# Gated linear attention, then a mixture of experts: key halves on array quarters, and forward scans that begin with reciprocals

## The chip, the core and the metric

The kernel runs on one core of a Trainium2 chip. A core has a matrix engine (TensorE, PE in the tables), a vector engine (VectorE, DVE), a scalar engine (ScalarE, ACT), a general engine (GpSimd, POOL) and a queue that only issues transfers (SyncE, SP). Each runs its own list of instructions in order, and they wait for each other through semaphores. The metric is the time of one execution on the device in microseconds: before the change the median of three runs is 389.31 us (389.28 to 391.26). All data is 32-bit floating point unless a sentence says otherwise.

## What is computed

First a gated linear attention over 4 batches, 8 heads, 768 steps and heads of 48, then a hierarchical mixture of 16 experts over the 3072 resulting rows.

```python
for t in range(S):
    state = alpha[:, :, t, :, None] * state + np.einsum('bhd,bhe->bhde', k[:, :, t], v[:, :, t])
    y[:, :, t] = np.einsum('bhd,bhde->bhe', q[:, :, t], state)
...
g_idx = np.argmax(x @ w_group, axis=1)      # one of 4 groups, then one of its 4 experts
...
h = np.maximum(xg[mask_e] @ w1[g, e], 0.0)
out[tok_idx] = combined[:, None] * (h @ w2[g, e])
```

The recurrence is computed in chunks of 128 steps. Within a chunk the keys are multiplied by the product of the decays that still follow them (a scan that runs backwards gives these products), the queries by the product of the decays so far (a scan that runs forwards), and the causal part of queries times keys, times the values, gives the chunk's own share. A state of 48 by 48 for each head carries the rest from chunk to chunk. Since both factors are counted towards the chunk's end, the queries have to be divided by the product over the whole chunk.

## The kernel before

There are 24 chunks (4 batches of 6). The 8 heads lie in 4 pairs: a pair fills 112 partitions, one head on 0 to 47, the other on 64 to 111. The host has the inputs laid out so. The inputs come in 11 units of one, two or three chunks, each cut in two or four parts; for the later batches a part is one pair over three chunks, so its rows are 3 x 128 = 384 elements long (387 with a boundary element for each chunk). A part of two chunk-pairs has 256 (258).

For each part (names as the planner has them):

- R, `back` (L378): the backward scan on DVE. Its second operand is a column of ones in PSUM (`one_col`).
- KP, `decayed` (L414): keys times the scan, on POOL, or on DVE where `BY_DVE` (L709) lists the part.
- F, `forth` (L388): the forward scan on DVE. Its second operand is `starts`, a tile that occupies a whole PSUM bank: 3e38 everywhere but 1.0 at the chunks' beginnings, so that a multiply followed by a minimum begins anew with each chunk.
- W, `wholes` (L395, L396): for each unit a reciprocal of the whole-chunk products and a minimum.
- QS, `queries` (L405): ACT multiplies the queries by that reciprocal, one instruction for each pair and chunk, 128 elements each.
- QP (L414): scaled queries times the forward scan, on POOL or DVE.

For each chunk, on PE:

- SC, `scores` (L428): 8 products of 128 keys by 128 queries, contraction 48, into two PSUM banks.
- masks: head set by head set, either DVE multiplies the PSUM bank by a triangle of ones (`masked`, L433), or ACT copies the bank to SBUF (L856) and POOL blanks the upper triangle (`mask`, L437). `MASKS` (L891) says how many of the two DVE takes.
- OUT, `outputs` (L506): masked scores times values, contraction 128, on top of FB, `from_before` (L494): queries times the state.
- G, `gains` (L463), with the keys turned by TR (L446): what the chunk adds to the state; DVE adds it (L472) and ACT scales it (L479).
- ROWS, `to_rows` (L527): the outputs turned to rows, with the router's logits beside them.

Then DVE chooses the experts for groups of chunks, and POOL scatters each chunk's 128 rows to the experts' slots with one indirect DMA (X, L625). When all rows are there, the experts run one after the other: L237 is the first matrix product, L248 the second. The rows of a job are fetched by SP, turned on DVE (L1031), and the results sent out by POOL (L1023).

The order of instructions on each engine is fixed when the program is built. `in_turns` (L35) is a list scheduler: every piece of work has an engine, a duration that was written in by hand, the pieces that it needs and a due time; the engines' queues are filled in the order it finds. PE's pieces are in a fixed sequence of their own. `FIRST` and `STEP` (L704) set the due times of the chunks, `X0` and `XSTEP` (L892) those of the scatters, `QUEUE` (L788) the order of SP's transfers: L a unit's inputs, V values, W the weights of ROWS, B the filling of the slots. `cq`, the forward scan's result, has three buffers, so a forward scan waits until the product QP three parts earlier has read its buffer.

Of the kernel before, what the change touches and what calls it, by code (L numbers as in the profile page):

```python
# [12 lines left out]
F32 = mybir.dt.float32  # L13
# [9 lines left out]
P = 128  # L23
# [11 lines left out]
def in_turns(works, free):  # L35
# [19 lines left out]
    while len(turns) < len(works):  # L55
# [7 lines left out]
        for w in sorted((w for t, w in can if t <= now + 1e-9), key=lambda w: w.due):  # L63
            if not any(now < t < now + w.takes - 0.4 and y.due < w.due and y.due < now + w.takes
                       for t, y in can):
                w.start, free[e] = now, now + w.takes
                left[e].remove(w)
                turns.append(w)
                break
# [27 lines left out]
def gla_then_hierarchical_moe(  # L97
# [71 lines left out]
    def bank():  # L169
# [9 lines left out]
    causal = cp.tile([P, P], F32, name="causal")  # L179
    nc.gpsimd.memset(causal, 1.0)  # L180
    nc.gpsimd.affine_select(out=causal, in_=causal, pattern=[[1, P]], compare_op=ALU.is_ge,
                            fill=0.0, base=0, channel_multiplier=-1)
# [78 lines left out]
    nc.vector.memset(starts[0:R, 0:UC * A1:A1], 1.0)  # L261
# [7 lines left out]
    with ExitStack() as gla:  # L269
# [42 lines left out]
        for kind, u, i, n in blocks_of(units, HP):  # L312
            begins[kind, u, i] = at
            at += P * width_of(kind, n)

# [67 lines left out]
        def forth(u, i):  # L383
# [5 lines left out]
                out=cq, data0=a[:, 0:n * A1], data1=starts[0:R, 0:n * A1], initial=1.0,  # L389
                op0=ALU.mult, op1=ALU.min)  # L390

        def wholes(u):
            k = units[u][2]
            ready["whole", u] = w = sp.tile([R, HP, UC], F32, name="whole")
            nc.vector.reciprocal(out=w[:, :, 0:k], in_=ready["rev", u][:, :, :, 0])  # L395
            nc.vector.tensor_tensor(out=w[:, :, 0:k], in0=w[:, :, 0:k],  # L396
                                    in1=starts[0:R, 1:2, None].to_broadcast([R, HP, k]),
                                    op=ALU.min)

        def queries(u, i):  # L400
            n, q, _, _ = of_unit(u, i)
            k, g = units[u][2:]
            for j in range(n):
                c = j % k
                nc.scalar.activation(out=q[:, j, :], in_=q[:, j, :], func=AF.Copy,  # L405
                                     scale=ready["whole", u][:, i * g + j // k, c:c + 1])

        def decayed(kind, u, i, engine):
# [3 lines left out]
            else:  # L412
                of, by = q, ready.pop(("cq", u, i)).rearrange("r (c s) -> r c s", c=n)
            engine.tensor_tensor(out=part_of(kind, u, i, P), in0=of, in1=by[:, :, 1:A1],  # L414
                                 op=ALU.mult)

        def side(p, i):

            c = (i + p + 1) % 2
            return slice(64 * c, 64 if c == 0 else R)  # L420

        def scores(n):
            u, c = where[n]
            qp, kp = ready["qp", u], ready["kp", u]
            z = [pairs.tile([P, HP, P], F32, name=f"zs{i}") for i in range(2)]
            for p in range(HP):
                for i, r in enumerate(heads):
                    nc.tensor.matmul(z[i][:, p, :], lhsT=kp[r, p, c, :],  # L428
                                     rhs=qp[r, p, c, :], start=True, stop=True)
            return z  # L430

        def masked(sm, z, i):
            nc.vector.tensor_tensor(out=sm[:, i], in0=z[i], in1=causal[:, None, :]  # L433
                                    .to_broadcast([P, HP, P]), op=ALU.mult)

        def mask(sm, i):
            nc.gpsimd.affine_select(  # L437
                out=sm[:, i], in_=sm[:, i], pattern=[[0, HP], [1, P]],
                compare_op=ALU.is_ge, fill=0.0, base=0, channel_multiplier=-1)
# [43 lines left out]
        def of(z, p):  # L483
            return z[:, p % 2, p // 2 * P:(p // 2 + 1) * P]

        def from_before(n, st):
# [4 lines left out]
            for p in range(HP):  # L491
                for i, r in enumerate(heads):
                    o = side(p, i)
                    nc.tensor.matmul(of(z, p)[o], lhsT=st[r, p, 0:o.stop - o.start],  # L494
                                     rhs=qp[r, p, c, :], start=(p < 2), stop=False,
# [3 lines left out]
        def outputs(n, sm, z):  # L499
# [3 lines left out]
            for i in range(2):  # L503
                for p in range(HP):
                    h, o = 2 * p + i, side(p, i)
                    nc.tensor.matmul(of(z, p)[o],  # L506
# [799 lines left out]
```

## Time and profile before

The profiled execution took 390.5 us, of which 388.8 us are the span from its first instruction to its last. The table is taken from that execution.

| row of the profile | instructions | busy us | mean ns |
|---|---|---|---|
| PE, all | 3366 | 374.7 | |
| PE, experts, L237 and L248 | 1536 | 252.8 | 325 |
| PE, scores L428 | 384 | 28.2 | 285 |
| PE, outputs L506 | 384 | 27.2 | 280 |
| DVE, all | 420 | 162.4 | |
| DVE, mask of 512 elements from PSUM, L433 | 28 | 18.3 | 679 |
| DVE, forward scans L388 of 387 elements (w, qka) | 16 and 8 | 15.0 and 7.5 | 945, 947 |
| DVE, forward scans L388 of 258 elements (qka, w) | 6 and 6 | 4.1 and 4.0 | 677, 674 |
| ACT, all | 379 | 139.3 | |
| ACT, scaling of queries L405 (w, qka) | 60 and 36 | 19.8 and 11.7 | 402, 407 |
| ACT, copies of scores L856 | 20 | 11.0 | 576 |
| POOL, all | 240 | 195.3 | |
| POOL, blanking of 512 elements L437 | 20 | 12.5 | 637 |

Each f32 matrix product appears as two instructions, so the 8 products of a chunk's scores are 16. The busy time of PE counts the whole latency of overlapping instructions, so a busy PE says little about how much of the array is used; the distance from one group's start to the next says more. The granted clock of PE is 0.992 of full speed over the span.

The attention takes the first 117 us or so of the span and the experts almost all of the rest: the last OUT starts at 115.17 us, the first full expert job (216 columns) at 141.47 us, and the last expert's second product ends at about 378 us.

### The profile page before, as it was taken

What the parts mean: (1) busy time and instruction counts of PE and PEld (TensorE: products, weight loads), DVE (VectorE), ACT (ScalarE), POOL (GpSimd) and SP (SyncE); (2) the same over time, 40 slices, a digit from 0 to 9 for tenths busy, and PEclk for the clock granted to TensorE, in tenths of its full rate; (3) what the DMA queues carried; (4) which work ended last, traced back from release to release, by engine and by line L of the source; (5) the groups of instructions that cost most, each with busy time, mean ns of one, the idle gap of its engine ahead of it and who ended that gap; (6) DMA issues with size and microseconds to landing.
All of it is one profiled execution on the core that took longest, in us unless ns stands there. A gap on an engine that the chain in (4) does not pass through costs nothing.

```text
span 388.8 us, 8864 instructions
## 1 busy us (share of the span) xinstructions
PE 374.7 (96%) x3366; PEld 356.6 (92%) x3366; DVE 162.4 (42%) x420; ACT 139.3 (36%) x379; POOL 195.3 (50%) x240
## 2 busy tenths in 40 slices
PE   8999999999999899999999999999999999999990
PEld 3888998898989899999999999999999999999990
DVE  7999998899868220207322020220201202202200
ACT  5989899596762211111121121211212112112110
POOL 5988886888746321244261633526336235144341
PEclk9999999999999999999999999999999999999996
DMA  8999999994313799986585866768668777665000
GB/s 284 380 410 412 413 358 352 410 417 172 100 64 128 154 328 346 333 244 219 175 255 218 276 220 207 224 227 282 227 201 257 269 245 240 249 250 182 16 22 27
DMA packets 32411, 95.22 MB, mean 245 GB/s; under 512 B 18175, under 2 KB 18454, under 8 KB 27888
## 3 DMA queue, kind: packets, MB, share of 16 engines
q1 hardware_dynamic: 27552, 85.10, 63.5%
q0 software_dynamic: 4816, 9.55, 7.3%
q8 instruction: 27, 0.44, 0.5%
q14 instruction: 16, 0.13, 0.1%
HBM read 79.47 MB, written 15.56 MB: 244 GB/s over the span
## 4 chain that ended last, share of the span: by engine, by line
PE 69%; DMA 18%; issue 5%; POOL 4%; SPq 1%; DVE 1%; POOLq 0%; ACT 0%; DVEq 0%; ACTq 0%
PE bank L237 29%; PE bank L248 29%; DMA slots_d<-blank 7%; DMA qka<-in_qka_dram 5%; DMA w<-in_qka_dram 3%; PE zo L506 3%; PE zs L428 3%; PE bank L527 2%; DMA out_dram<-yq,dst_q 2%; POOL out_dram L1023 1%; DMA v<-in_v_dram 1%; PE zo L494 1%; SPq L320 1%; POOL slots_d L625 1%; PE bank L446 1%
## 5 line engine op out<-in xcount | busy, mean ns | idle before, releaser
L1023 POOL DMA_INDIRECT out_dram<-yq,dst_q x99 | 96.4, 974 | 153.2 <-DVE yq L1019 121.3
L237 PE MATMUL bank<-xt_e,w 128*128 128x128 f32 (+15 forms) x768 | 126.5, 325 | 1.4 <-DVE dst_q L1045 0.8
L248 PE MATMUL bank<-hT,w 128*128 128x128 f32 (+15 forms) x768 | 126.3, 324 | 0.0
L237 PEld LDWEIGHTS bank<-xt_e,w 128*128 128x128 f32 x768 | 124.1, 190 | 1.7 <-PE bank L248 0.9
L248 PEld LDWEIGHTS bank<-hT,w 128*128 128x128 f32 x768 | 124.1, 190 | 0.0
L1040 DVE CAST dst_q<-xq 128x7 int32<-128x7 f32 (+2 forms) x16 | 2.7, 168 | 168.8 <-DMA out_dram<-yq,dst_q 168.8
L239 ACT ACTIVATE hT<-bank 128x256 f32<-128x256 f32 (+15 forms) x64 | 31.3, 489 | 96.3 <-PE bank L237 96.3
L250 ACT COPY yT<-bank 128x256 f32<-128x256 f32 (+31 forms) x32 | 12.7, 398 | 109.0 <-PE bank L248 109.0
L625 POOL DMA_INDIRECT slots_d<-xr,place x24 | 24.1, 1002 | 10.6 <-issue 3.3
L506 PE MATMUL zo<-sm,v 128*48 128x128 f32 (+1 forms) x384 | 27.2, 280 | 1.0 <-POOL sm L437 1.0
L428 PE MATMUL zs<-qp,kp 48*128 48x128 f32 x384 | 28.2, 285 | 0.0
L527 PE MATMUL bank<-wr,yt 112*128 112x116 f32 x192 | 26.1, 279 | 0.5 <-ACT sm L856 0.5
L506 PEld LDWEIGHTS zo<-sm,v 128*48 128x48 f32 (+1 forms) x384 | 20.3, 129 | 6.5 <-POOL sm L437 2.4
L428 PEld LDWEIGHTS zs<-qp,kp 48*128 48x128 f32 x384 | 23.4, 187 | 2.6 <-DVE qp L414 0.8
L527 PEld LDWEIGHTS bank<-wr,yt 112*128 112x128 f32 x192 | 23.3, 191 | 0.9 <-ACT sm L856 0.7
L405 ACT ACTIVATE w<-w,whole 112x128 f32<-112x128 f32 x60 | 19.8, 402 | 2.0 <-DMA w<-in_qka_dram 2.0
L378 DVE TENSOR_TENSOR_SCAN rev<-w,starts 112x387 f32<-112x387 f32 (+1 forms) x22 | 18.5, 869 | 3.4 <-DMA w<-in_qka_dram 3.4
L414 POOL TENSOR_TENSOR kp<-w,rev 112x384 f32<-112x384 f32 (+1 forms) x21 | 18.3, 886 | 2.2 <-DVE rev L378 2.0
L414 POOL TENSOR_TENSOR qp<-w,cq 112x384 f32<-112x384 f32 (+1 forms) x20 | 17.1, 862 | 4.4 <-ACT w L405 3.9
L433 DVE TENSOR_TENSOR sm<-zs,causal 128x512 f32<-128x512 f32 x28 | 18.3, 679 | 2.4 <-PE zs L428 2.2
L388 DVE TENSOR_TENSOR_SCAN cq<-w,starts 112x387 f32<-112x387 f32 (+1 forms) x22 | 19.1, 871 | 0.0
L1016 DVE STREAM_TRANSPOSE yq<-yT 128x672 f32<-128x672 f32 (+2 forms) x15 | 12.3, 818 | 15.5 <-ACT yT L250 15.4
(135 smaller groups left out, 340.6 us busy)
## 6 DMA issues: line engine op xcount, KB each, us to landing
w<-in_w_dram SPq DMA_DIRECT2D x32, 1536.0 KB, 7.1
w<-in_qka_dram SPq DMA_DIRECT2D x16, 578.0 KB, 10.4
slots_d<-blank SPq DMA_DIRECT2D x4, 1372.0 KB, 19.1
qka<-in_qka_dram SPq DMA_DIRECT2D x8, 578.0 KB, 12.7
v<-in_v_dram SPq DMA_DIRECT2D x3, 1152.0 KB, 15.8
xq<-slots_d SPq DMA_DIRECT2D x32, 85.8 KB, 7.6
qka<-in_qka_dram SPq DMA_DIRECT2D x6, 385.5 KB, 6.3
xq<-slots_d SPq DMA_DIRECT2D x28, 73.5 KB, 6.3
```

Source lines behind the costliest of these rows:

```text
L237: nc.tensor.matmul(z[:, k * n:(k + 1) * n], lhsT=w1[:, dc, f * P:(f + 1) * P], rhs=xt[:, dc, 0:n], start=(dc == 0), stop=(dc == DC - 1))
L239: return lambda: nc.scalar.activation(out=hT[:, f0:f0 + 2, 0:n], in_=z[:, 0:2 * n].rearrange("p (f t) -> p f t", f=2), func=AF.Relu)
L248: nc.tensor.matmul(z[:, i * n:(i + 1) * n], lhsT=w2[:, f, dc * P:(dc + 1) * P], rhs=hT[:, f, 0:n], start=(f == 0), stop=(f == FC - 1))
L378: nc.vector.tensor_tensor_scan(out=part_of("rev", u, i, A1).rearrange("r c s -> r (c s)")[:, ::-1], data0=a[:, W:0:-1], data1=one_col.to_b ...
L388: nc.vector.tensor_tensor_scan(out=cq, data0=a[:, 0:n * A1], data1=starts[0:R, 0:n * A1], initial=1.0, op0=ALU.mult, op1=ALU.min)
L405: nc.scalar.activation(out=q[:, j, :], in_=q[:, j, :], func=AF.Copy, scale=ready["whole", u][:, i * g + j // k, c:c + 1])
L414: engine.tensor_tensor(out=part_of(kind, u, i, P), in0=of, in1=by[:, :, 1:A1], op=ALU.mult)
L428: nc.tensor.matmul(z[i][:, p, :], lhsT=kp[r, p, c, :], rhs=qp[r, p, c, :], start=True, stop=True)
L506: nc.tensor.matmul(of(z, p)[o], lhsT=vs[b][:, bc, h * D:h * D + o.stop - o.start], rhs=sm[:, i, p, :], start=(p < 2 and bc == 0), stop=Tru ...
L527: nc.tensor.matmul(z[:, at:at + W], lhsT=yt[:, p, :], rhs=wr[:, p, :], start=(p == 0), stop=(p % 2 == 1), skip_group_check=True)
L625: dma = nc.gpsimd.indirect_dma_start(out=slots_by[cs.start + c], out_offset=bass.IndirectOffsetOnAxis(ap=it["to"][:, c:c + 1], axis=0), in ...
L1023: nc.gpsimd.indirect_dma_start(out=out_by.popleft().rearrange("n (j w) -> (n j) w", j=4), out_offset=bass.IndirectOffsetOnAxis(ap=dst[:, b ...
```

## The change

Seven things are changed together.

1. SC computes the keys of a chunk in two halves of 64. The first pass multiplies one half with all 128 queries, the second the other half with the last 64 queries alone; the quarter of the scores that is always zero is not computed. Each product uses 64 rows and 64 columns of the array, and four neighbouring products in the order lie on four different quarters.
2. The scores of a head set now take 384 columns of a bank: 256 whose keys and queries belong to the same half (they need the triangle), then 128 that need none. Masks multiply the 256 alone, on DVE or on POOL (a product with the triangle in place of the blanking), and ACT copies the rest.
3. OUT too is done by key halves on quarters, with a `drain` of PE before the first pass (where FB came before it) and between the two passes.
4. The queries are no longer scaled: QS goes, and W writes reciprocals for two parts at a time into `begun`, a new SBUF tile that takes the place of `starts` as the second operand of the forward scans. So a forward scan begins with the reciprocal, and now needs W, and W the backward scans of its parts.
5. G moves behind ROWS, next to FB; before it stood behind OUT.
6. The layout follows: values of half of the heads come with the two halves of a chunk swapped, keys of those parts are written with the halves swapped, and the pairs are distributed over the two output banks in another way.
7. The plan is new: other durations, `MASKS`, `BY_DVE`, `QUEUE`, groups, due times, and 0.2 in place of 0.4 in a rule of the scheduler. Eight products KP and QP lie on DVE in place of four. The fill B 0 now goes ahead of unit 7's inputs, and unit 8's inputs come after the values V 2.

The core of the diff:

```diff
-    causal = cp.tile([P, P], F32, name="causal")
+    HB, HS = P // 2, HP // 2
+    halves = [slice(0, HB), slice(HB, P)]
+    causal = cp.tile([P, HB], F32, name="causal")
...
-    nc.vector.memset(starts[0:R, 0:UC * A1:A1], 1.0)
...
+        begun = buf.tile([R, 2, UC * A1], F32, name="begun")
+        nc.vector.memset(begun, HUGE)
...
             nc.vector.tensor_tensor_scan(
-                out=cq, data0=a[:, 0:n * A1], data1=starts[0:R, 0:n * A1], initial=1.0,
+                out=cq, data0=a[:, 0:n * A1], initial=1.0,
+                data1=begun[:, i % 2, 0:n * A1],
                 op0=ALU.mult, op1=ALU.min)
...
-        def wholes(u):
-            k = units[u][2]
-            ready["whole", u] = w = sp.tile([R, HP, UC], F32, name="whole")
-            nc.vector.reciprocal(out=w[:, :, 0:k], in_=ready["rev", u][:, :, :, 0])
...
-        def queries(u, i):
...
-                nc.scalar.activation(out=q[:, j, :], in_=q[:, j, :], func=AF.Copy,
-                                     scale=ready["whole", u][:, i * g + j // k, c:c + 1])
+        def wholes(u, j):
+            _, _, k, g = units[u]
+            of = ready["rev", u][:, 2 * g * j:2 * g * (j + 1), :, 0]
+            nc.vector.reciprocal(out=begun[:, :, 0:g * k * A1:A1],
+                                 in_=of.rearrange("r (i g) c -> r i (g c)", g=g))
...
+        def by_quarters(j):
+            for m in range(HS):
+                for p in (m, m + HS) if j == 0 else (m + HS, m):
+                    yield p, slice(0, P) if j == 0 else halves[1], lies(p, j)
...
-            z = [pairs.tile([P, HP, P], F32, name=f"zs{i}") for i in range(2)]
-            for p in range(HP):
-                for i, r in enumerate(heads):
-                    nc.tensor.matmul(z[i][:, p, :], lhsT=kp[r, p, c, :],
-                                     rhs=qp[r, p, c, :], start=True, stop=True)
+            z = pairs.tile([P, 2, 512], F32, name="zs")
+            for j in range(2):
+                for p, qs, x in by_quarters(j):
+                    for i, r in enumerate(heads):
+                        nc.tensor.matmul(blocks(z[x, i, 0:3 * HS * HB], p, j),
+                                         lhsT=kp[r, p, c, x],
+                                         rhs=qp[r, p, c, qs].rearrange("r (a q) -> r a q", q=HB),
+                                         start=True, stop=True)
...
+        def only_earlier(engine, to, z):
+            k = z.shape[1]
+            to, z = (t[:, :, 0:OWN].rearrange("s i (a q) -> s i a q", q=HB) for t in (to, z))
+            engine.tensor_tensor(out=to, in0=z, in1=causal[:, None, None, :]
+                                 .to_broadcast([P, k, 2 * HS, HB]), op=ALU.mult)
...
+            for j in range(2):
+                if j or bc:
+                    nc.tensor.drain()
+                for p, qs, x in by_quarters(j):
+                    for i in range(2):
+                        h, o = 2 * p + i, side(p, i)
+                        nc.tensor.matmul(of(z, p)[o, qs].rearrange("r (a q) -> r a q", q=HB),
+                                         lhsT=vs[b][x, bc, h * D:h * D + o.stop - o.start],
+                                         rhs=blocks(sm[x, i], p, j),
...
-            add(f"W{u}", DVE, 0.34, 0.42, partial(wholes, u), each("R", u),
+            for j in range(parts(u) // 2):
+                add(f"W{u}.{j}", DVE, 0.2, 0.28, partial(wholes, u, j),
+                    each("R", u)[2 * j:2 * j + 2], before_it("F", u, 2 * j))
...
-        QUEUE = [('L', 1), ('V', 0, 0, 1), ('L', 2), ('L', 3), ('W',), ('V', 0, 1, 3), ('L', 4), ('V', 0, 3, 6), ('L', 5), ('L', 6), ('V', 1, 0, 6), ('L', 7), ('L', 8), ('V', 2, 0, 6), ('B', 0), ('B', 1), ('B', 2), ('B', 3), ('L', 9), ('V', 3, 0, 6), ('L', 10)]
+        QUEUE = [('L', 1), ('V', 0, 0, 1), ('L', 2), ('W',), ('V', 0, 1, 3), ('L', 3), ('L', 4), ('V', 0, 3, 6), ('L', 5), ('L', 6), ('V', 1, 0, 6), ('B', 0), ('L', 7), ('V', 2, 0, 6), ('L', 8), ('B', 1), ('B', 2), ('B', 3), ('L', 9), ('V', 3, 0, 6), ('L', 10)]
...
-        MASKS = [1, 0, 0, 1, 1, 1, 0, 2, 0, 0, 1, 1, 1, 2, 1, 2, 2, 2, 2, 2, 2, 2, 1, 1]
+        MASKS = [1, 1, 0, 1, 1, 1, 0, 0, 1, 1, 1, 1, 1, 1, 2, 2, 2, 2, 2, 2, 2, 1, 1, 1]
```

## The prediction, made before the changed kernel had run

> **What bounds the kernel now.** I read the page first, then the chain of waits, PE's timeline, and busy time by stretches. The experts fill PE from 141 us on and the change touches none of them. What is at stake is the attention, up to about 117 us. From 75 us on the chain of waits there is PE alone, one group after another, and earlier PE's timeline shows the same groups with gaps of 0.7 us at most. One chunk on PE:
>
> ```profile
> 105.58 0.66 PE L494 MATMUL zo<-qp,state 48*48 48x128 f32 x16
> 106.17 1.09 PE L506 MATMUL zo<-sm,v 128*48 128x128 f32 x16
> 107.08 0.64 PE L463 MATMUL bank<-v,kt 128*48 128x48 f32 x16
> 107.64 1.16 PE L428 MATMUL zs<-qp,kp 48*128 48x128 f32 x16
> 108.74 0.60 PE L446 MATMUL bank<-ident,kp 112*128 112x112 f32 x4
> 109.18 1.06 PE L527 MATMUL bank<-wr,yt 112*128 112x116 f32 x8
> 110.17 0.74 PE L494 MATMUL zo<-qp,state 48*48 48x128 f32 x16
> ```
>
> Start to start: FB 0.59, OUT 0.91, G 0.56, SC 1.10, TR 0.44, ROWS 0.99, together 4.59 us. OUT runs from 9.74 us (chunk 0) to 115.17 us (chunk 23), 4.58 us a chunk: PE sets the pace. But the others have little room (columns: stretch, its length, then PE, PE's weight loads, DVE, ACT, POOL, each busy us with its count):
>
> ```profile
> 5.00:20.00 15.00, 14.48 (x185) 10.79 (x185) 14.57 (x36) 12.15 (x36) 12.98 (x25) 1.00 1.03 386
> 20.00:60.00 40.00, 39.67 (x631) 34.97 (x628) 38.29 (x76) 36.44 (x113) 33.51 (x43) 1.00 1.02 396
> 60.00:101.00 41.00, 40.30 (x641) 35.92 (x643) 37.29 (x97) 31.20 (x96) 33.58 (x37) 1.00 0.80 311
> ```
>
> DVE is busy 90.2 of these 96 us, POOL 80.1, with 15.9 us of gaps. The preparation (scans and products) ends here: the last QP ends at 100.9, and SC of chunk 21, the first that needs it, starts at 102.9, so the lead is 2.0 us.
>
> **PE.** Within a group the trace has one quarter of the array taking a 128-column matmul each 0.109 us (FB: 105.724, 105.834, 105.943). Streaming alone is then FB 4 x 0.109 = 0.44, OUT 8 x 0.109 = 0.87, G 0.47, SC 8 x 0.112 = 0.89, TR 0.39, ROWS 0.89, sum 3.95. The missing 0.64 lies at the four places where the array changes its shape (ROWS to FB, FB to OUT, G to SC, SC to TR): 0.16 each. After: SC and OUT each have 4 x 0.109 in the first pass and 4 x 0.058 in the second (G's pitch for 64 weight columns), 0.67, so streaming is 3.53. FB, OUT and SC share one shape, and three changes remain: 0.48. Two drains come. Neither occurs before: at least 0.16 each, as a change of shape empties the array too; at most 0.32, if a drain also waits for the modelled end (272 ns of a matmul less its 109 ns) before that. I take 0.24. Sum 3.53 + 0.48 + 0.48 = 4.49, a gain of 0.10 a chunk, **2.4 us** over 24; by the ends 6 us gained or 1.4 us lost.
>
> Here a rule speaks against the change. The Trainium skill, "TensorE: Matmul & The Clock Gate", section "Wait — 56ns, not 53.3ns?", says that starts of matmuls never come closer than about 25 ns, however small. SC and OUT become 32 instructions each: 0.80 in place of 0.67, 0.26 a chunk, 6 us in all, and the gain is a loss of 3.8. The row says otherwise where quarters differ: FB's first four start at 105.578, .584, .591 and .598, 7 ns apart. G's 16 take 28 ns each, but there weights set the pitch. I take the row.
>
> **ACT.** QS goes: 19.8 + 11.7 = 31.5 us. Copies of scores were 11.0; now 14 of 384 elements (the row of XR, 0.48), 3 of 768 (0.84, the row of the 784-element copy), 14 of 128 (about 0.28, between EX's 60 elements at 0.26 and 192 at 0.33) and 7 of 256 (0.385) give 15.9. Net -26.6 us, and none of it on the path at once; what it removes are POOL's waits for ACT's queries, 3.9 + 2.1 = 6.0 us.
>
> **DVE.** Masks 18.3 us become 14 of 256 (0.40, the DVE product's row) and 7 of 512 (0.68): 10.4. Reciprocals: 10 pairs, 3.5 us, become 18 of about 0.19: 3.4. Products: four more, +1.6. `begun`'s memset (0.7) lies in the 1.6 us before the first input. Net -6.4 us, worth nothing while PE sets the pace.
>
> **POOL.** Own work up to the last QP: 48 products of 384 at 0.895 (two in a row took 1.79) = 43.0, 16 of 256 at 0.64 = 10.2, masks 11 x 0.64 + 3 x 1.25 = 10.8 (POOL has no such row; its product of 256 is nearest, doubled for 512), 13 scatters ahead of that QP in the new order at 1.19 (12.30 us for 12, and 0.16 gaps) = 15.5, constants 0.6. Sum 80.1, as before.
>
> **The forward scans' second operand.** It moves from PSUM to SBUF, and this is what I think decides. Columns: start, duration.
>
> ```profile
> 59.18 0.95 DVE L388 TENSOR_TENSOR_SCAN cq<-w,starts 112x387 f32<-112x387 f32 x1
> 59.31 0.95 POOL L414 TENSOR_TENSOR kp<-w,rev 112x384 f32<-112x384 f32 x1
> ...
> 14.90 0.64 POOL L414 TENSOR_TENSOR kp<-w,rev 112x256 f32<-112x256 f32 x1
> 15.44 0.40 DVE L414 TENSOR_TENSOR qp<-w,cq 112x256 f32<-112x256 f32 x1
> 15.49 0.93 POOL L414 TENSOR_TENSOR kp<-w,rev 112x256 f32<-112x256 f32 x1
> ```
>
> A scan with its second operand in PSUM and a POOL product run side by side, each at its usual time. But where DVE runs a product with both inputs in SBUF, POOL's product of 0.64 takes 0.93: it stood for 0.29 of the 0.34 us that the two overlap. At 24.27 the other order shows: POOL's product runs, and DVE's takes 0.58. The Trainium skill, "SBUF — State Buffer", section "Who interferes with whom", states it as a rule: a DVE instruction with two SBUF inputs contends with a GpSimd instruction that reads SBUF, and the later one waits until the earlier has finished. By the rule every scan holds POOL for its whole length; by the row for 0.85 of the overlap.
>
> The scans' pitch is 0.875 (24 wide) and 0.61 (12): 28.3 us, and eight DVE products bring 2.9, together 31.2. By the row's 0.85 that is 26.5, by the rule 31.2; I take the row. Scatters read no rows on POOL that the scan could hold, as far as the trace tells, and the 7.6 us of scans that fall among scatters (69 to 101) lie beside them half of the time: 3.8 free. **22.7 us** remain to be served one after the other. POOL's gaps were 15.9, of which 6.0 went with QS; its longest one (3.25 us, up to 69.2) is the first scatter waiting for the fills to land, which a later POOL meets already landed, so most of the other 9.9 vanish too, and I leave 2. The last QP then ends at 4.9 (first product) + 80.1 + 22.7 + 2 = 109.7 against 100.9: +8.8. Less the lead of 2.0 that is eaten first, and 0.3 for three faster chunks after it: **+6.5 us** at the end of the attention. DVE suffers too: a scan finds POOL at work two times in three and waits some 0.4, and with three `cq` buffers it also waits for the delayed QP; its own 6.4 us pay for that.
>
> **Ends of the attention.** The first SC needs QP of the second part, at 7.9 us before; in the new order POOL's QP of the first part stands against the second scan and a DVE product, and it comes at 7.5 to 8: nothing. Behind the last OUT the chain is gates, last scatters, rows, expert 0; it follows the last OUT, so a shift of that one arrives whole. SP: fill B 0 (1.4 MB, 3.5 us at 390 GB/s) now stands ahead of unit 7's inputs, which landed at 40.4 and are scanned at 44.7; V 2 and it delay unit 8's by 6.5, scanned at 52.5 but used at 76. Neither reaches PE; without that lead it would be 3.5 us.
>
> **Sum.** 389.3 + 6.5 = **395.8 us** for the median; the profiled execution, 390.5 with a span of 388.8, would be near 397.
>
> **Rivals.**
>
> - *Faster: PE keeps the pace.* Scans don't hold POOL, or the holds fall into gaps that lie ahead of need (units 6 to 9 were ready 3 to 6 us early). For it: 15.9 us of gaps and a lighter DVE. Then 389.3 - 2.4 = 386.9; with the cheap drain 383.1. It decides if less than 14 of the 22.7 us remain: the last QP then comes by 100.8, when a PE that gained 0.10 a chunk is ready for it (102.9 less 2.1). Chance 0.27.
> - *No difference:* the hold eats the lead and PE's gain, 387.4 to 391.3. Chance 0.13 with the weak end of my forecast.
> - *Much slower: DVE and POOL hold each other,* by the whole rule, with all 9.9 us of gaps kept: +4.7 + 7.9 on top, 408. Against it: they would have to miss every gap. Chance 0.05 above 403.
> - *The change doesn't do what it says:* quarters run two at a time. SC becomes 16 x 0.109 / 2 + 16 x 0.058 / 2 = 1.34, OUT the same, +0.67 each, 32 us: 421. FB's four at once speak against it. Chance 0.01.
>
> My forecast holds 0.54, from 391.3 to 403. Within 0.5% (1.9 us) I call no difference, which is about what a measurement of this kernel can tell. Slower 0.60, same 0.13, faster 0.27. Range 385 to 403: 0.12 lie below it, 0.06 above.
>
> **What would show it.** Right: L388's scans or POOL's products grow from their usual 0.95 and 0.92 to 1.2 and more where they overlap; the last QP ends near 110; PE has gaps before SC that end at a product. Wrong: those rows stay, and PE's chunk is 4.5 us or less throughout. PE's part alone: SC start to next start near 0.83, OUT to SC near 0.91. If PE's chunk without waits is above 4.6, the drains cost over 0.3 each and the first rival falls too.

## The result: 5.3% slower, and the profile after

The changed kernel takes 411.95 us (median of four runs, 407.02 to 414.40) against 389.29 us before; the ratio is 1.053, with an interval of 1.045 to 1.061. The forecast was 395.8 us: the sign was right, the size less than a third of it. The profiled execution took 414.4 us, of which 412.3 us are the span: 23.5 us more than before. It was the slowest of the four and counts as a slow one, with a mean clock of 0.961; the other three took 407.0 to 412.1 us at 0.965 to 0.983, so what is read from the clock below holds for this one execution. All of the added time lies in the attention. OUT of the last chunk starts at 138.88 us in place of 115.17, and behind it the experts take the time that they took. A chunk now takes 5.60 us in place of 4.58.

The same stretches as before (stretch, length, then PE, PE's weight loads, DVE, ACT, POOL, each busy us with its count; then the granted clock, the busy share of the DMA engines, GB/s):

```profile
5.00:20.00 15.00, 11.46 (x236) 8.37 (x235) 13.40 (x29) 4.88 (x14) 8.55 (x16) 1.00 1.03 378
20.00:60.00 40.00, 33.97 (x728) 27.87 (x728) 35.93 (x69) 21.86 (x63) 35.86 (x36) 0.96 1.02 399
60.00:101.00 41.00, 37.95 (x675) 31.39 (x674) 27.11 (x63) 17.32 (x51) 26.63 (x27) 0.71 0.73 272
```

Two things are new. PE is no longer busy all the time, though nobody else is busier: between 60 and 101 us DVE fell from 37.3 to 27.1 us and POOL from 33.6 to 26.6. And the clock of PE, 1.00 in the whole attention before, is 0.96 and 0.71. The row of the page that gives it in 40 slices of the span (9 is 90% or more) shows where:

```profile
PEclk9999895589999999999999999999999999999997
```

By the trace's record of the clock it is at half speed from 41.8 to 45.2 us and from 62.2 to 86.1 us, and full elsewhere in the attention. At half speed a chunk on PE takes some 6.4 to 6.8 us.

The step that the forecast took as decisive is there, and as large as forecast:

```profile
L396 DVE TENSOR_TENSOR_SCAN cq<-w,begun 112x387 f32<-112x387 f32 x16 | 20.1, 1273 | 0.0
L419 POOL TENSOR_TENSOR qp<-w,cq 112x384 f32<-112x384 f32 x16 | 18.2, 1148 | 3.7 <-DVE cq L396 2.7 <-DVE lg L560 0.9
L419 POOL TENSOR_TENSOR kp<-w,rev 112x384 f32<-112x384 f32 x16 | 17.9, 1126 | 5.2 <-DVE rev L386 5.2
```

These forward scans of 387 elements last 1.27 us in place of 0.945 (the eight that read another tile 1.44 in place of 0.947), these products of POOL 1.13 to 1.15 in place of 0.92 to 0.94, while the backward scans, which still read PSUM, stay at 0.93. All forward scans together take 40.8 us in place of 30.8, POOL's products of both sizes 10.8 us more than the same number took before, and the eight products on DVE about 1.5 us more (0.41 to 0.67 us each; before, three of four took 0.40 to 0.42). Together some 22 us are spent holding and waiting; the forecast said 22.7. But the last QP ends at 125.1 us, not at 109.7.

What had no place in the forecast shows in the timeline of PE (start, duration; in brackets the idle time before, and what ended it):

```profile
58.59 0.95 PE L554 MATMUL bank<-wr,yt 112*128 112x116 f32 x7
61.09 0.26 PE L554 MATMUL bank<-wr,yt 112*128 112x116 f32 x1 [1.56 <-issue]
```

ROWS has eight matmuls with one wait ahead of the first. Seven run, then PE stands still for 1.56 us, and then comes the eighth, which waits for nothing and nobody. "issue" says just that: no releaser.

### The profile page after: what moved, and what is told of

It reads as the page before. It is cut to its first block, busy times and chain, and to the rows that moved or that the text cites. A ratio compares the mean times of both kernels' runs of the same rounds, so it can differ in the third digit from the quotient of the medians.

```text
span 412.3 us, 10329 instructions
## 1 busy us (share of the span) xinstructions
PE 383.1 (93%) x4134; PEld 358.0 (87%) x4134; DVE 168.2 (41%) x413; ACT 116.4 (28%) x301; POOL 206.9 (50%) x234
## 4 chain that ended last, share of the span: by engine, by line
PE 69%; DVE 9%; issue 7%; POOL 7%; DMA 4%; ACT 2%; SPq 1%; POOLq 0%; DVEq 0%; ACTq 0%
PE bank L242 27%; PE bank L253 27%; PE zo L532 4%; PE bank L554 4%; DVE cq L396 4%; PE zs L449 3%; POOL qp L419 2%; DMA w<-in_w_dram 2%; POOL kp L419 2%; PE zo L516 1%; PE bank L468 1%; PE bank L485 1%; DVE rev L386 1%; POOL out_dram L1058 1%; SPq L1185 1%
## 5 line engine op out<-in xcount | busy, mean ns | idle before, releaser
L532 PEld LDWEIGHTS zo<-sm,v 64*48 64x48 f32 (+1 forms) x768 | 20.2, 137 | 20.2 <-issue 13.0
L532 PE MATMUL zo<-sm,v 64*48 64x64 f32 (+3 forms) x768 | 29.8, 272 | 8.1 <-DVE sm L460 2.4
L554 PE MATMUL bank<-wr,yt 112*128 112x116 f32 x192 | 30.0, 305 | 2.6 <-issue 1.6
L449 PE MATMUL zs<-qp,kp 48*64 48x128 f32 (+1 forms) x768 | 25.1, 262 | 4.0 <-POOL qp L419 2.6
L554 PEld LDWEIGHTS bank<-wr,yt 112*128 112x128 f32 x192 | 26.6, 215 | 1.8 <-ACT yt L541 1.7
L449 PEld LDWEIGHTS zs<-qp,kp 48*64 48x64 f32 x768 | 21.8, 146 | 5.7 <-POOL qp L419 4.3
L419 POOL TENSOR_TENSOR qp<-w,cq 112x384 f32<-112x384 f32 (+1 forms) x21 | 22.2, 1068 | 8.9 <-DVE cq L396 7.9
L396 DVE TENSOR_TENSOR_SCAN cq<-w,begun 112x387 f32<-112x387 f32 (+1 forms) x22 | 24.1, 1116 | 0.1
L460 POOL TENSOR_TENSOR sm<-sm,causal 128x256 f32<-128x256 f32 (+1 forms) x17 | 14.6, 859 | 13.6 <-ACT sm L883 11.6
L541 ACT COPY yt<-zo 112x512 f32<-112x512 f32 x24 | 14.0, 582 | 24.0 <-PE zo L532 24.0
L501 ACT ACTIVATE state<-gained,rev 112x48 f32<-112x48 f32 x64 | 16.2, 324 | 8.7 <-DVE gained L494 8.6
## 6 DMA issues: line engine op xcount, KB each, us to landing
w<-in_qka_dram SPq DMA_DIRECT2D x16, 578.0 KB, 10.7
slots_d<-blank SPq DMA_DIRECT2D x4, 1372.0 KB, 17.7
```

The lines of the kernel that those rows point to most:

```text
L396: nc.vector.tensor_tensor_scan(out=cq, data0=a[:, 0:n * A1], initial=1.0, data1=begun[:, i % 2, 0:n * A1], op0=ALU.mult, op1=ALU.min)
L419: engine.tensor_tensor(out=to, in0=of, in1=by, op=ALU.mult)
L449: nc.tensor.matmul(blocks(z[x, i, 0:3 * HS * HB], p, j), lhsT=kp[r, p, c, x], rhs=qp[r, p, c, qs].rearrange("r (a q) -> r a q", q=HB), sta ...
L501: nc.scalar.activation(out=st[:, p, 0:D], in_=sums[:, p], func=AF.Copy, scale=ready["rev", u][:, p, c, 0:1])
L532: nc.tensor.matmul(of(z, p)[o, qs].rearrange("r (a q) -> r a q", q=HB), lhsT=vs[b][x, bc, h * D:h * D + o.stop - o.start], rhs=blocks(sm[x ...
L554: nc.tensor.matmul(z[:, at:at + W], lhsT=yt[:, p, :], rhs=wr[:, p, :], start=(p == 0), stop=(p % 2 == 1), skip_group_check=True)
```

## Two candidates for the missing 16 us

All records of PE (one for each instruction in the trace: weight loads, products, drains and semaphore instructions) can be counted from the start of the program. In the first profile of the changed kernel the stalls inside a group, without a wait and without a drain, stand at the records 705, 1729, 1985, 3009 and 3521. Each is 193 beyond a multiple of 256. The queues of the page (packets, MB, share) say what comes in such portions, first before, then after:

```profile
q8 instruction: 27, 0.44, 0.5%
```
```profile
q8 instruction: 33, 0.54, 0.6%
```

33 packets of 16 KB for 8422 records of PE, 27 for 6845: one packet brings 256 instructions. The Trainium skill, "Runtime: NRT & Kernel Launch", section "Instruction fetch mechanics", says the same of the blocks (16 KB, 256 instructions), and that crossing from one to the next is mostly hidden. Here it is hidden before and not after. The packets' own times in the trace of the changed kernel:

| block begins with record | block before it entered at | DMA share since | packet starts, takes | PE goes on at | stall, start to start |
|---|---|---|---|---|---|
| 705 | 18.9 | 1.02 | 22.29, 1.11 | 24.9 | 0.80 |
| 1729 | 46.9 | 1.02 | 50.29, 1.43 | 52.8 | 0.63 |
| 1985 | 52.8 | 1.03 | 58.65, 0.93 | 61.1 | 1.82 |
| 3009 | 86.9 | 1.03 | 90.49, 0.95 | 92.8 | 0.44 |
| 3521 | 99.1 | 0.59 | 102.01, 1.68 | 105.3 | 0.81 |
| 4033 | 111.0 | 0.14 | 112.23, 1.00 | 115.6 | none |

By these times a block seems to be fetched when PE enters the one before it. With the queues full of data the packet starts 3 to 4 us later, once 5.9, takes 0.9 to 1.7 us, and PE goes on 1.1 to 1.6 us after its end: 5.8 to 6.2 us in all, once 8.3. PE's records per chunk rose from about 152 to 216 and two drains, so ahead of the late blocks 256 of them were used up in 5.2 to 6.5 us, where in the attention before they lasted 6.8 to 9.2. Before the change no block came late.

So there were two theories for what the forecast lacked: (A) the hold between scans and products is worth far more than its 22.7 us, since late products starve PE; (B) PE itself is the bound, through the arrival of its instructions and the drains, and the half clock follows any long gap. The first experiments were written with (A) in mind, the later ones with both.

## The experiments

Each ratio is to the kernel before on the same chip, with its interval. That kernel took 398.3 us beside four of them (the second operand in PSUM as first tried, the hold alone, a drain alone, idle work), where its clock was 0.978 to 0.988, and 389.5 beside the others. No trace of it shows what it lost on that chip, so sizes from these four are less sure.

### The second operand back in PSUM

```diff
-                data1=begun[:, i % 2, 0:n * A1],
+                data1=starts[0:R, 0:n * A1],
...
-            of = ready["rev", u][:, 2 * g * j:2 * g * (j + 1), :, 0]
-            nc.vector.reciprocal(out=begun[:, :, 0:g * k * A1:A1],
+            of = ready["rev", u][:, g * i:g * (i + 1), :, 0]
+            nc.vector.reciprocal(out=starts[0:R, 0:g * k * A1:A1],
```

> The changed kernel with the second operand of the forward scans back in PSUM: the reciprocals of one part at a time are written into the columns of the bank that held it before, so W becomes 36 instructions in place of 18. Theory (the scans in SBUF and POOL's products hold each other, POOL comes late, PE starves, and only then its clock falls to half): forward scans back to 0.95 us, POOL's products of 384 to 0.92, clock 1.00 in the whole attention, PE's chunk 4.66 us in place of 4.59, so 389.3 + 24 x 0.07 = 391, 388 to 394. Rival 1 (PE itself: drains and the new order of its groups cost the time): scans fall back, the time stays above 404. Rival 2 (the clock falls because half-filled arrays don't keep it up, starved or not): scans fall back, the clock still drops to 0.5 for 20 us, time about 400.

Measured: 434.7 us, ratio 1.089 (1.081 to 1.098), above 404 as the first rival had it. The hold is gone, yet by its ratio the kernel is slower than the changed one, and (A) has lost its simple form:

```profile
L394 DVE TENSOR_TENSOR_SCAN cq<-w,starts 112x387 f32<-112x387 f32 x16 | 15.2, 947 | 0.2
L417 POOL TENSOR_TENSOR kp<-w,rev 112x384 f32<-112x384 f32 x16 | 14.9, 936 | 1.9 <-DVE rev L384 1.8
```

PE's clock is at half speed in five stretches, 61.4 us together. Each follows gaps of PE, four of them a gap of 1.4 us or more. The planner had put the 36 W in other places, and the first chunk already waited 2.6 us for its mask. With W in another order this was not the changed kernel minus one part, so it was made again, with every engine in the changed kernel's order:

```diff
+            if i % 2:
+                nc.vector.tensor_copy(out=starts[0:R, 0:n * A1:A1], in_=firsts[:, 0:n])
...
-                data1=begun[:, i % 2, 0:n * A1],
+                data1=starts[0:R, 0:n * A1],
...
+            for i, to in (0, starts[0:R, 0:g * k * A1:A1]), (1, firsts[:, 0:g * k]):
+                of = ready["rev", u][:, g * (2 * j + i):g * (2 * j + i + 1), :, 0]
+                nc.vector.reciprocal(out=to, in_=of.rearrange("r g c -> r (g c)"))
```

> The changed kernel in its own order on every engine; only the forward scans read their second operand from PSUM again. W writes the reciprocals of the first part there and those of the second into a small tile, from which a copy of three elements brings them before the second scan (some 6 us more for DVE in all). If the hold between scans and POOL's products is the main loss: scans 0.95, last QP 8 us or more earlier, 10 to 14 us faster than the changed kernel on this chip (ratio to before 1.02 or less). If the stalls of PE and the half clock after them are the main loss: scans 0.95 too, but the ratio stays within 0.01 of the changed kernel's or rises.

The unchanged kernels ran beside it:

> The kernel before, unchanged, for its profile on this chip: ratio 1.00 to itself. If stalls of PE without a releaser and a half clock belong to the changed kernel alone, it has none here; if a chip has them whatever the kernel, they show here too.

> The changed kernel, unchanged, on the same chip as the others: about 1.05 times before. In its first profile five stalls of PE without wait or drain came at PE's instructions 705, 1985, 3009 and the like, all 193 beyond a multiple of 256. If that is a limit of how the instructions arrive, they fall again on such numbers and on no others; if it was chance, elsewhere.

Measured: before 389.7 us, 1.001 (0.999 to 1.003); the changed kernel 414.3 us, 1.061 (1.056 to 1.065); without the hold 407.4 us, 1.049 (1.041 to 1.057). By the ratios the hold is worth 1.2% here, about 5 us, with an interval of 1 to 8 (DVE's 6 us of additional work counted against it). But the four runs without it spread from 401.7 to 412.4 us, and the two faster ones, 401.7 and 406.6, lie 10 us below the changed kernel's median. So it is 5 to 10 us, between the two expectations. The profiled execution without the hold was the fastest (400.0 us of span) and has no half clock before the experts' end, with the same half-filled arrays: these alone do not halve the clock. Still its last OUT starts at 126.8 us in place of 115.2, and 11.6 us are lost with neither hold nor half clock. What remains in it is this, seven times between 24 and 95 us:

```profile
48.82 0.84 PE L450 MATMUL zs<-qp,kp 48*64 48x128 f32 x26
50.52 0.34 PE L450 MATMUL zs<-qp,kp 48*64 48x64 f32 x6 [0.86 <-issue]
```

The stalls stand at the records 705, 1729, 1985, 2241, 2497, 3009 and 3521, again all 193 beyond a multiple of 256, 0.66 to 1.23 us each from start to start, 6.9 together. In the repeat of the changed kernel they stand at 705, 1729, 1985 and 3009 (1.10, 1.07, 2.99 and 0.73); 3521 came without one. The kernel before has none above 0.2 in its repeat. That settles where the stalls come from; the lines of the program at these records differ from kernel to kernel, the count does not.

The four runs without the hold also say what the half clock costs: 401.7, 406.6, 408.1 and 412.4 us with a mean clock of 0.991, 0.983, 0.967 and 0.964. From the first to the last the clock takes away 11.2 us more of the span, and the time grew by 10.7; to the two between them it takes 3.3 and 9.8 us more, and the time grew by 4.8 and 6.4.

### The hold alone, in the kernel before

```diff
+        begun = buf.tile([R, UC * A1], F32, name="begun")
+        nc.vector.memset(begun, HUGE)
+        nc.vector.memset(begun[:, 0:UC * A1:A1], 1.0)
...
-                out=cq, data0=a[:, 0:n * A1], data1=starts[0:R, 0:n * A1], initial=1.0,
+                out=cq, data0=a[:, 0:n * A1], data1=begun[:, 0:n * A1], initial=1.0,
```

> The kernel before with one edit: the second operand of the forward scans, same values, lies in an SBUF tile in place of the PSUM bank. Theory (the hold between scans and POOL's products): scans 1.2 us and more where they meet a product, the attention 8 to 15 us longer, and PE's clock dips once PE waits. Rivals (drains, the new plan, the half arrays): 389 to 391, scans 0.95.

Measured: 411.1 us, 1.036 (1.030 to 1.043), about 14 us on that chip. As the theory said:

```profile
L392 DVE TENSOR_TENSOR_SCAN cq<-w,begun 112x387 f32<-112x387 f32 x16 | 21.9, 1373 | 0.0
L418 POOL TENSOR_TENSOR kp<-w,rev 112x384 f32<-112x384 f32 x16 | 16.4, 1039 | 2.3 <-DVE rev L382 2.3
```

The last QP ends at 114.2 us in place of 100.4 to 100.9. So the hold can cost more than the whole forecast where the rest leaves it no room. In the changed kernel PE is late anyhow, and part of the hold probably lies beside that; no run separates the two.

### The reciprocals alone, without the hold

```diff
-                add(f"QS{u}.{i}", ACT, 0.293 * n, 0.293 * n + 0.12, partial(queries, u, i),
-                     [f"W{u}"] + ([] if u else ["Lq"]))
...
+            nc.vector.reciprocal(out=starts[0:R, 0:g * k * A1:A1],
+                                 in_=of.rearrange("r g c -> r (g c)"))
```

> The kernel before with one part of the change alone: the queries are not scaled, and each forward scan begins with the reciprocals, but written into the PSUM bank that held its second operand (one small reciprocal for each part). ACT loses 31.5 us of work, DVE gains some 3. PE's records per chunk stay 152. Theory (the idea costs nothing, its place in SBUF did): scans 0.95 us, ratio 0.995 to 1.005, no stall of PE between instruction blocks. Rival (a forward scan that must wait for its backward scans is itself the loss): 1.01 and more, PE waits for QP.

Measured: 390.8 us, 1.001 (0.995 to 1.006), no half clock, no late block. The idea of beginning a scan with reciprocals costs nothing, and 31.5 us less for ACT bring nothing. It is the place of the operand that costs.

### A drain alone

```diff
             for i in range(2):
+                if i:
+                    nc.tensor.drain()
                 for p in range(HP):
```

> The kernel before with one drain of PE in each chunk, between the two passes of OUT (24 in all). PE has hardly a gap there, so each drain counts. At the forecast's 0.24 us: 389.3 + 24 x 0.24 = 395.1. At the 0.36 read from the changed kernel's trace: 397.9. At the low end, 0.16: 393.1. If drains cost nothing beyond what waits hide: 389 to 390.

Measured: 402.3 us, 1.011 (1.006 to 1.016), some 4 us for 24 drains; the change has 44. In the trace a chunk with nothing late shows the price:

```profile
94.78 1.38 PE L508 MATMUL zo<-sm,v 128*48 128x128 f32 x16
96.00 0.62 PE L463 MATMUL bank<-v,kt 128*48 128x48 f32 x16
96.55 1.16 PE L428 MATMUL zs<-qp,kp 48*128 48x128 f32 x16
97.64 0.60 PE L446 MATMUL bank<-ident,kp 112*128 112x112 f32 x4
98.08 1.06 PE L529 MATMUL bank<-wr,yt 112*128 112x116 f32 x8
99.07 0.66 PE L494 MATMUL zo<-qp,state 48*48 48x128 f32 x16
99.66 1.38 PE L508 MATMUL zo<-sm,v 128*48 128x128 f32 x16
```

From OUT to OUT 4.88 us in place of 4.59: a drain costs 0.29 us. That would be 7 us; the medians differ by 4, with an interval of 2.4 to 6.5. Why it is less isn't shown; the kernel before was 9 us slower on this chip to begin with.

### More and smaller products alone

```diff
             for p in range(HP):
-                for i, r in enumerate(heads):
-                    nc.tensor.matmul(z[i][:, p, :], lhsT=kp[r, p, c, :],
-                                     rhs=qp[r, p, c, :], start=True, stop=True)
+                for x in slice(0, 64), slice(64, P):
+                    for i, r in enumerate(heads):
+                        nc.tensor.matmul(z[i][x, p, :], lhsT=kp[r, p, c, x],
+                                         rhs=qp[r, p, c, :], start=True, stop=True)
```

(and ROWS in the same way)

> The kernel before with SC and ROWS issued as twice as many products of half the keys or rows (SC 8 to 16, ROWS 4 to 8 a chunk); same results, same order, no drain, everything else as before. PE's records per chunk rise from 152 to 200 (216 in the changed kernel), its streaming time should stay (two halves of the array side by side). If the arrival of PE's instructions limits: stalls at numbers 193 beyond a multiple of 256, clock dips behind the longer ones, 5 us and more slower than before. If the number of instructions is of no matter: ratio 1.00 to 1.005.

Measured: 397.5 us, 1.018 (1.012 to 1.024), 7 us for nothing but more instructions. The array itself takes no longer: from FB to FB a chunk with nothing late takes 4.58 us, as before.

```profile
102.55 0.66 PE L495 MATMUL zo<-qp,state 48*48 48x128 f32 x16
107.13 0.66 PE L495 MATMUL zo<-qp,state 48*48 48x128 f32 x16
```

The loss comes with two late blocks, at the records 1985 (0.85 us) and 2241:

```profile
62.98 0.41 PE L495 MATMUL zo<-qp,state 48*48 48x128 f32 x3
66.69 0.65 PE L495 MATMUL zo<-qp,state 48*64 48x128 f32 x13 [3.29 <-issue]
```

The packet of that block started 7.2 us after the block before was entered (57.1 and 64.3 us). Behind the gap the clock is halved from 67.7 to 71.1 us:

```profile
68.00:71.00 3.00, 3.00 (x43) 2.34 (x40) 0.08 (x1) 0.65 (x2) 0.00 (x0) 0.50 0.86 307
```

### Fewer transfers in flight

```diff
+            for name in in_queue[7:][-2:-1]:
+                tc.add_manual_dep(dma.ins, name, mybir.DependencyInfo(
+                    mybir.DependencyClass.Sync, mybir.DependencyReason.DATA),
+                    reason="two in flight")
```

(in the changed kernel with the second operand in PSUM)

> The changed kernel with the second operand in PSUM (as the run a_psum2), and at most two of SP's transfers in flight in place of some eight. In the traces a block of 256 PE instructions is fetched by one packet of 16 KB that starts 3.2 to 4 us after the block before it was entered while the transfers fill the queues, 6.8 us among the fills, and 0.6 to 1.2 us where few run. If it waits behind the queued data: below 3 us now, stalls between blocks below 0.4 us each in place of 0.7 to 1.2, last OUT near 122 us in place of 127, ratio 1.02 to 1.03. If the delay doesn't come from queued data: stalls as before. If the inputs then come too late: gaps of DVE at its scans and a ratio above 1.05.

Measured: 426.2 us, 1.081 (1.072 to 1.090). As a remedy it fails: inputs come too late, as the last of the expectations had it, and the clock is halved for 47.8 us. For the mechanism it says what was asked. All seven late blocks come in time. Those at 705, 1729, 1985, 2241 and 2497 do so with the DMA share at 0.72 to 0.88, their packets starting 1.2 to 2.1 us after the block before was entered; at 3009 and 3521 PE itself was slow or the packet early. Two others, 2753 and 4033, are late by 1.6 and 1.9 us, with the DMA share at 1.02 and 0.98 and packets that start 4.8 and 4.2 us after. So the packet does wait behind queued data.

### The order of SP's transfers

(`QUEUE` as before the change, in the changed kernel)

> The changed kernel with the order of SP's transfers from before. Theory: the order is of no matter, ratio to before 1.055 to 1.065 as for the changed kernel. Rival (the early fill and the late inputs of unit 8 cost time, or set the long stall of PE at 61 us): 1.045 or less, and no stall above 1.5 us.

Measured: 412.2 us, 1.056 (1.049 to 1.063), as the changed kernel's 1.061 (1.056 to 1.065) within the intervals; the block at 1985 comes 2.5 us late here too. The order is of no matter that could be measured.

### Keeping PE's clock up with idle work

```diff
+            for _ in range(DUMMIES if 5 <= n < 18 else 0):
+                nc.tensor.matmul(starts[:, 0:3 * P], lhsT=ones,
+                                 rhs=ones[:, None, :].to_broadcast([P, 3, P]), start=True, stop=True)
```

> The changed kernel with three idle bf16 products (128 x 128 weights, 384 columns, into unused columns of a PSUM bank, read by nobody) ahead of SC in chunks 5 to 17, which only keep the array busy; about 0.8 us a chunk at full clock. If the half clock is a cost of its own, set off by starving: the clock over 60 to 101 us rises from 0.71 to above 0.95, and the time falls by 5 to 10 us, to 400 to 405. If the clock only marks the waiting and POOL still sets the pace: no gain, 410 to 414. If PE's own work sets the pace: slower by 13 x 0.8 = 10 us, above 418.

Measured: 428.3 us, 1.076 (1.071 to 1.081). The clock is 1.00 from 60 to 101 us, but half from 41.8 to 55.5 and again from 137 us, and the added 0.8 us a chunk is lost. By its ratio it is 6 to 9 us slower than the changed kernel, as was expected if PE's own work sets the pace. It tells little more: filling work moves the half clock and costs more than it saves.

### The three costs together, in the kernel before

(the edits of the hold, of the smaller products and of the drain, the latter before and between the passes of OUT)

> The kernel before with the three suspected costs added and nothing of the change's gains: the forward scans' second operand in SBUF, SC and ROWS as twice as many products, a drain before and between the passes of OUT. Apart, they cost 3.6, 1.75 and (one drain) 1.1%. If these three make up the change's loss: 1.055 to 1.08, with scans of 1.3 us, stalls at instruction blocks and a half clock behind the longer ones, as in the changed kernel (1.061). If each merely fills the same waits: 1.04 to 1.05, and something else in the change costs the rest.

Measured: 407.8 us, 1.045 (1.039 to 1.051), in the range expected if something else in the change costs the rest. A late block is there as in the changed kernel, and forward scans of 387 elements last 1.13 to 1.25 us:

```profile
55.02 0.50 PE L468 MATMUL bank<-v,kt 128*48 128x48 f32 x12
59.18 0.40 PE L468 MATMUL bank<-v,kt 128*64 128x48 f32 x4 [3.67 <-issue]
```

Apart, the three cost 3.6, 1.8 and 1.1% (with one drain). Together they cost less than their sum, probably since they fill the same waits of PE (two of the three were measured on the slower chip). Some 18 us of the changed kernel's 23 to 25 are remade with them. What this kernel lacks is the long half clock: 7 us of it, against 27 and 31 us in the two profiles of the changed kernel. At half speed, 20 to 24 us more of it take 10 to 12 us of PE's time, enough for the remaining 5 to 7. That it is this which costs them is argued, not shown: the new masks, the place of G and the other order of work were never run alone.

## Why the prediction was too small

**What was right.** The sign and the mechanism that it put first: scans and products hold each other, some 22 us measured against 22.7, and the +6.5 us that it made of this is within what taking the hold away gave back (5 to 10). It was wrong about who pays: the forecast laid nearly all on POOL, and the trace has 10.0 us on the scans and 10.8 on POOL's products. ACT's copies come to 15.5 us (forecast 15.9) and DVE's masks to 10.5 (10.4). POOL's masks are somewhat longer, 0.77 and 1.27 us (0.64 and 1.25). SP's order costs nothing. And quarters of the array do run four at a time: the first pass of SC starts four products every 0.109 us, the second every 0.058, as the sum had it.

**The step that failed** is PE's: "Sum 3.53 + 0.48 + 0.48 = 4.49, a gain of 0.10 a chunk, **2.4 us** over 24". Two things are wrong with it. The smaller is a size. A chunk of the changed kernel without waits:

```profile
115.06 0.86 PE L449 MATMUL zs<-qp,kp 48*64 48x128 f32 x32
115.86 0.60 PE L468 MATMUL bank<-ident,kp 112*128 112x112 f32 x4
116.29 1.06 PE L554 MATMUL bank<-wr,yt 112*128 112x116 f32 x8
117.28 0.67 PE L485 MATMUL bank<-v,kt 128*64 128x48 f32 x16
117.88 0.67 PE L516 MATMUL zo<-qp,state 48*48 48x128 f32 x16
118.68 1.23 PE L532 MATMUL zo<-sm,v 64*48 64x128 f32 x32
119.72 0.52 PE L449 MATMUL zs<-qp,kp 48*64 48x128 f32 x12
```

SC to TR takes 0.80 (forecast 0.83), but OUT to SC 1.04 (0.91) and FB to OUT 0.80 (0.44 + 0.24). Each is 0.12 us or a little more above the forecast; laid on its drain alone, that makes 0.36 us a drain, above the upper end of 0.32. The chunk is 4.66 us, a loss of 0.07 in place of a gain of 0.10; over 24 chunks 4 us of the error. By the forecast's own test ("If PE's chunk without waits is above 4.6, the drains cost over 0.3 each and the first rival falls too") the faster case was gone with this.

The larger is what the sum left out: how PE's instructions arrive. It added up the time of the array and took for granted that PE is fed. Late blocks of the table came 5.8 to 6.2 us after the one before was entered. At some 6 us for 256 records, a chunk of 218 takes 218/256 x 6 = 5.1 us or more while the queues are full, which they are for most of the time up to 99 us; one of 152, as before, takes 3.6 and never met this bound. That is an estimate from the table. The trace has PE above it, not at it: from 18.9 to 52.8 us five blocks took 6.8 us each, 5.8 us a chunk, and only two of the five came late, so masks and products kept PE waiting too. Directly the five late blocks of this profile cost 4.5 us, seven without the hold 6.9. Alone, in the kernel before, the smaller products cost 7 us and 24 drains some 4, where the forecast had a gain of 2.4 us for all of PE's part.

**The clock.** The forecast took 1.00 throughout. In the profiled execution the mean clock of 0.961 takes 16.1 us of 412.3 away, against 3.1 before. In this trace it is a consequence of gaps. One stretch of half clock follows the late block at 59.5 us, the other a gap of 1.50 us that ends at a mask of DVE:

```profile
39.48 1.23 PE L532 MATMUL zo<-sm,v 64*48 64x128 f32 x32 [1.50 <-DVE sm L460]
```

From 31.5 to 39.5 us DVE and POOL are both busy all of the time; in the profile without the hold this gap is not there. An account by trace of the 23.5 us: half clock 13.0 more than before; the five late blocks 4.5; PE's own chunks 1.7; the rest, some 4, waits for masks, keys and products. These lie partly beside each other, and it is the account of the execution with the lowest clock. In the other three the clock takes only 3.8, 5.1 and 11.2 us more than before, and they are slower than before by 17.7, 22.8 and 22.5 us. So the half clock is not most of the loss in general; the runs show 5 to 10 us for the hold and 18 for the three causes together.

**The rivals.** Of those named none came true. "Much slower" was at 408 us by a full hold, and the time went past it for another reason. The range ended at 403 because two costs were not thought of, the supply of instructions and a clock below 1.00.

**A better version** was not found. Beginning the scans with reciprocals in PSUM keeps 389 to 391 us; the quarters as they are done here add records to PE in the stretch in which they come late.

## What to carry to other kernels

Count the instructions of the engine that sets the pace, not only its time: while transfers filled the queues, 256 instructions of PE took some 6 us to arrive here, and up to 8 and more, so cutting a product in two is not free even where the array would do both at once. Look in the trace for idle time that waits for nothing, inside a group, and count the records to it. And when a second operand moves from PSUM to SBUF, ask what runs beside it: beginning the scans with reciprocals cost nothing with the operand in PSUM, and the operand's move to SBUF alone cost 14 us.

## What was not expected of the hardware

- Late instruction blocks: packets of 16 KB on a queue of their own, 3 to 4 us from request to start with full queues, 7.2 and 8.0 us while the fills of the slots run (smaller products alone, three costs together), 1.2 us where they are nearly empty.
- A gap of some 1.5 us is enough to halve PE's clock up to 2.3 us later. Gaps of 1.50 and 1.56 us (changed kernel), 2.4 (one drain) and 3.3 (smaller products) did, and behind the first 8 us so did every gap of 1.32 us or more that began at full clock in the attention, in all these traces; of those around 1 us most did not, but one of 1.0 did (operand in PSUM as first tried, at 39 us), and two of 0.7 and 1.0 us close together (the hold alone, at 113 us). The Trainium skill, "TensorE: Matmul & The Clock Gate", section "HAM oscillation — how this bites in real kernels", warns of gaps above some 3.4 us; here less than half of that sufficed.
- How long the half clock lasts differs: 3.4 us with no drain and PE's groups in their old order (the hold alone, the smaller products alone), 6.8 us with the three costs together, 10.2 us with one drain a chunk, up to 23.9 us in the changed kernel, though PE is at work most of that time. Up to the experts every such stretch in the traces is a whole multiple of 3.41 us. Why it lasts so long is open.
- Some drains last far longer than their usual 0.6 to 1.2 us: 3.5 us at 104.0 us in the kernel with one drain a chunk, up to 3.4 us in the first one with the operand in PSUM, 2.5 us in that with idle work. Those far above the usual length all lay beside POOL's scatters; in the changed kernel itself drains beside scatters took their usual time. Left open.
